# One hand-written order of tasks against another in a fused attention and GeGLU kernel: the early blocks, and where ScalarE sums a load of x

## The chip, the cores and the metric

The kernel runs on one core of a Trainium2 chip. The core has TensorE (matrix products into PSUM), VectorE, ScalarE and GpSimd, which work side by side, and SyncE, whose queue issues the DMAs. In the profile they are PE (PEld for TensorE's weight loads), DVE, ACT, POOL and SP. Each engine works through its own list of instructions in order; semaphores hold an instruction back until what it needs is there. The metric is the device time of one execution in microseconds: 183.78 us for the kernel before, the median of three runs (183.71 to 183.88).

## The reference

The input x has 2048 rows of 512 bf16 numbers. All that follows is added to it.

```python
x = A_x
xn = _layernorm(x, axis=-1)
return x + _A_ref(xn, A_wqkv, A_wo) + _B_ref(xn, B_w_gate, B_w_up, B_w_down)
```

`_A_ref` is attention with 32 heads of 16 dimensions. A row attends to 8 rows: itself and those 2, 4, ... 14 before it.

```python
W, dil = 8, 2
idx = pos[:, None] - off[None, :]          # off = arange(W) * dil
logits = jnp.einsum("bhsd,bhswd->bhsw", q, kg) * scale
logits = jnp.where(mask[None, None, :, :], logits, -1e9)
attn = _softmax(logits, axis=-1)
o = jnp.einsum("bhsw,bhswd->bhsd", attn, vg)
... @ wo
```

`_B_ref` is a feed-forward part with 1376 hidden columns:

```python
h = _gelu(xn @ w_gate) * (xn @ w_up)
return h @ w_down
```

## The kernel before

The rows are worked in four blocks b = 0 to 3 of 512 rows, each of two loads p = 2b, 2b+1 of 256 rows (`ld_x0` to `ld_x7`; the two of block 0 that come first are split in halves). Every piece of work is a task with a name, and a table, `ORDER` (lines 363 to 420), lists for each engine its tasks in the order in which they are issued. `Graph` works out from what tasks read and write which of them must wait for which. A planner, `Graph.schedule` (line 168), runs through these lists with assumed durations; it does not change the order, but it gives each task its buffer: the buffer of a pool that is free first by the plan. For a DMA the plan takes `nbytes` over an assumed rate, a fixed part and `lat` (lines 244 to 249). The buffers that matter here are the 8 banks of PSUM (pool `P_ps`), one for each matmul group until it has been evicted.

The tasks of a block, by name (the number after the name is the block, then parts of it):

- **Layer norm.** For the first four loads VectorE makes the statistics (`bnst`, `bnag`, `sub`, `norm`, numbered by tile of 128 rows), ScalarE the square root (`sq`). From the fifth load on (tiles 8 to 15), ScalarE does it: `bnst` t sums a tile (line 736), `ve`, `vp` make the mean, `bnag` t sums the squares (line 782), `va`, `vb` the variance, GpSimd the square root (`sq8` to `sq14`), VectorE the reciprocal (`rstd`), and ScalarE `sub` (line 813) and `norm` (line 820). Tiles 8 and 9 come from `ld_x4`, 10 and 11 from `ld_x5`, 12 and 13 from `ld_x6`.
- **Transposing.** Block 0 on TensorE (`tpx`, `tpy`, evicted by `evx` on ScalarE and `evy` on VectorE), the others by DMA transposes on SP's queue (`trx`, line 860).
- **Query, key and value.** Block 0 in small pieces (`mma`, `mmb`, `mmt`, `mmv`), evicted by ScalarE (`evq0`, `evk0`, `evv0`); later blocks `mm`b_which_g with which = 0, 1, 2 (line 1035), evicted at line 1046. `halo` and `halv` carry the last 16 keys and values to the next block.
- **Attention.** VectorE multiplies queries and shifted keys (`pr`b_0, `pr`b_1, line 1066), adds (`pa`, and `pb` for blocks 1 to 3); TensorE sums over the dimensions of a head (`er`, lines 1102 and 1109, which also makes the last 96 up columns); `mask` for block 0; ScalarE copies the logits (`lc`, line 1138); VectorE takes the maximum and subtracts it (`d1a` to `d2`); ScalarE `exp`, VectorE sums (`d4a` to `d4c`), ScalarE `ln` and `d5`, VectorE `d6`. Four stores (`ss`) and four loads (`sl`) on SP's queue spread the probabilities through memory. VectorE multiplies values and probabilities (`pv`, line 1217), adds (`pw`) and finishes with `pz`.
- **Feed-forward.** `fg` and `fu` on TensorE (line 1255), ten each, and `fg`b_10; ScalarE evicts them with `gelu` (line 1265, and 1302 for the last) and `uev` (line 1272, and 1310 for the pieces `uev`b_10a, b, c); VectorE multiplies (`h`, line 1279, and 1317 for `h`b_10).
- **Output.** `acc` on TensorE (line 1347) adds both parts in PSUM, `fe` on ScalarE evicts, `fin` on VectorE adds x again (loaded by `ldxr`), `sto` stores.

ScalarE holds one set of function tables at a time: square root at first, then gelu, with exp and ln in between for each block; each change is an ACT_TABLE_LOAD row. A `ldxr` of block b is issued after `gelu`b_5 (`G.order_after`, line 1335).

Of the kernel before, what the change touches and what calls it, by code (L numbers as in the profile page):

```python
# [96 lines left out]
class Graph:  # L97
# [250 lines left out]
    def report(self):  # L348
# [14 lines left out]
ORDER = {  # L363
    "pe":
        "warm0 warm1 warm2 warm3 warm4 warm5 warm6 warm7 warm8 warm9 tpx0_0 tpy0_0 warm10 warm11 warm12 "
        "warm13 warm14 mma0_0 tpx0_1 tpy0_1 mmb0_0 mma0_1 mmb0_1 mmt1_1 tpx1_0 mmt1_0 mmt1_2 tpx1_1 mmt0_2 "
        "mmv0_0 mmt1_3 mmt0_3 mmv0_1 fg0_0 fg0_1 fu0_0 fg0_2 fg0_3 fu0_1 fu0_2 mm1_1_2_0 mmv1_0 mm1_1_0_0 "
        "mm1_1_1_0 fg0_4 fu0_3 mm1_0_1_0 fu0_4 mm1_0_0_0 er0_3 fg0_10 fg0_5 fu0_5 mm1_0_2_0 fg1_0 mm1_0_3_0 "
        "fu1_0 mm1_1_3_0 fg1_1 fu1_1 mm1_2_0_0 fg0_6 fg1_2 fu0_6 mm1_2_2_0 fg0_7 fu1_2 fg1_3 fu1_3 mm1_2_1_0 "
        "fu0_7 fg1_4 fg1_5 mmv1_1 fg1_6 fg0_8 mm1_2_3_0 fu1_4 fu1_5 fu0_8 fu1_6 fg1_7 er1_3 fg1_8 fg1_9 fg0_9 "  # L370
        "fu0_9 fu1_7 mm2_0_1_0 fu1_8 fu1_9 mm2_0_0_0 mm2_1_3_0 mm2_1_0_0 mm2_0_3_0 mm2_1_2_0 mm2_0_2_0 "
        "mm2_1_1_0 fg2_0 fu2_0 accd1 fg2_1 fu2_1 fg2_2 accd2 fg1_10 fg2_3 mm2_2_2_0 fu2_2 fg2_4 fg2_5 acca0 "
        "accb0 fu2_3 er2_3 fu2_4 fu2_5 accd3 fg2_10 mm3_1_0_0 fg2_6 mm3_2_2_0 fg2_7 mm3_0_1_0 mm3_1_1_0 fu2_6 "
# [3 lines left out]
        "fu3_9 acca8 accb8 accd9 accd10 acca12 accd15_1 accb12 accd15_0 accd14_0 accd11 accd13 accw15_0 "  # L377
        "accw13 accw15_1 accw14_0 accw12 accd14_1 accw14_1 accd15_2 accw15_2",
    "act":
        "c_tbl sx1 sq0 negm1 sxx1 evx0_0 sq1 evx0_1 sq2 evq0_0 evq0_1 evx1_0 sq3 evk0_1 evk0_0 evk0_2 evx1_1 "  # L380
        "sq6 bnst8 evq0_2 bnst9 sq4 ve8 evk0_3 vp8 evq0_3 bnag8 evv0_0_0 bnag9 gelu0_1 gelu0_2 va8 vb8 "
        "gelu0_0 gelu0_3 evv0_0_1 uev0_0 uev0_1 evk1_2_0 uev0_2 evk1_0_0 halo1 evv0_1_0 evk1_1_0 gelu0_4 "
        "bnst10 uev0_3 bnst11 evq1_1_0 ve10 uev0_4 vp10 evq1_0_0 bnag10 uev0_10c lc0 uev0_10a gelu0_5 bnag11 "
        "uev0_5 va10 uev0_10b bnst12 exp0 evk1_3_0 evq1_3_0 uev1_0 ln0 d5_0 evq1_2_0 gelu0_10 vb10 gelu1_2 "
        "gelu1_1 sub8 evv1_2_0 sub11 uev0_6 uev1_1 norm8 gelu1_0 uev1_3 gelu0_7 uev1_2 sub10 sub9 uev0_7 "
        "gelu1_3 gelu0_6 gelu1_4 evv1_0_0 evv1_1_0 evv0_1_1 norm11 gelu1_6 gelu1_5 gelu0_8 norm10 uev1_5 "
        "bnst13 uev1_4 norm9 ve12 vp12 uev0_8 lc1 uev1_6 bnag12 bnag13 gelu0_9 uev0_9 gelu1_7 uev1_7 gelu1_9 "
        "gelu1_8 bnst14 va12 uev1_8 vb12 halv1 evv1_3_0 uev1_9 evq2_1_0 evk2_0_0 exp1 evq2_0_0 halo2 evk2_2_0 "
        "evq2_2_0 evk2_1_0 evk2_3_0 ln1 sub12 halv2 bnst15 ve14 vp14 uev1_10b evq2_3_0 fe1 d5_1 sub13 bnag14 "
        "bnag15 va14 vb14 halo3 uev1_10c uev2_0 gelu2_1 gelu2_2 norm12 sub15 evv2_2_0 sub14 fe2 gelu2_0 "  # L390
# [6 lines left out]
        "fe9 fe10 fe11 fe13 fe12",  # L397
    "dve":
        "c_wdz bnst0 bnag0 sub0 rstd0 norm0a norm0b mean1 sub1 evy0_0 rstd1 norm1a norm1b bnst2 bnag2 evy0_1 "
        "sub2 rstd2 norm2 bnst3 bnag3 sub3 rstd3 norm3 bnst7 bnst6 bnag7 bnag6 bnst4 sub6 rstd6 bnst5 norm6 "  # L400
        "bnag5 bnag4 sub7 sub5 rstd4 norm5 sub4 norm7 norm4 pr0_0 pr0_1 pa0 rstd8 h0_0 h0_1 mask d1a_0 d1b_0 "
        "d1c_0 d2_0 pr1_0 d4a_0 d4b_0 d4c_0 h0_2 d6_0 pr1_1 h0_10 pa1 h1_0 rstd10 pb1 h0_3 h1_1 pv0_0 pv0_1 "
        "d1a_1 h1_2 d1b_1 pw0_1 d1c_1 h0_4 d2_1 h1_4 pw0_2 d4a_1 pz0 d4b_1 d4c_1 h1_3 pr2_0 d6_1 pr2_1 fin1 "
        "rstd12 pa2 fin2 rstd14 pb2 h1_10 pv1_1 d1a_2 pv1_0 d1b_2 fin3 d1c_2 fin0 d2_2 h2_1 pw1_1 d4a_2 h2_10 "
        "h2_2 d4b_2 h2_0 d4c_2 pw1_2 d6_2 pz1 pr3_0 pr3_1 h2_3 pa3 pb3 fin5 pv2_0 d1a_3 d1b_3 d1c_3 d2_3 "
# [5 lines left out]
        "sq8 sq10 sq12 sq14",  # L411
    "sp":
        "ld_x0_0 ld_x0_1 ld_wq ld_x1_0 ld_wk ld_x3 ld_x1_1 ld_x2 ld_wv ld_x4 ld_wg0 ld_wu0 trx3_0 trx2_1 "
        "trx2_0 trx3_1 ld_wu1 ld_wg1 ld_wt0 ld_x5 ld_wt1 ld_wt2 ld_x6 ld_wd0 ldxr1 ss0_2 ss0_1 ss0_3 ss0_0 "
        "sl0_1 sl0_0 ld_x7 ld_wd1 trx4_0 sl0_3 ldxr2 ld_wo sl0_2 trx5_1 trx4_1 trx5_0 ss1_3 ss1_0 ss1_1 ss1_2 "
        "sl1_3 sl1_1 trx6_0 sl1_2 sl1_0 trx7_1 ldxr3 trx7_0 trx6_1 ldxr0 ldxr4 ss2_0 ss2_1 ss2_3 sto2 ss2_2 "
        "sl2_3 sl2_0 sto0 ldxr5 sl2_1 ldxr13 sto3 ldxr12 sl2_2 ldxr8 ldxr6 sto5 ldxr7 ldxr10 ss3_3 ss3_0 "
        "ss3_2 ss3_1 sl3_1 sl3_0 sl3_2 sl3_3 ldxr9 ldxr11 sto1 ldxr14 sto7 sto4 ldxr15 sto6 sto8 sto9 sto10 "
# [20 lines left out]
def bass_parallel_sum__sliding_local_dilated__glu_gated_geglu__prompt_kernel(nc, A_x, A_wqkv, A_wo, B_x, B_w_gate, B_w_up, B_w_down, out, dbg=None, cfg=None):  # L439
# [43 lines left out]
    with contextlib.ExitStack() as es:  # L483
        block = es.enter_context(nc.Block())

        def sb(name, shape, dt):
            return es.enter_context(nc.sbuf_tensor(name, shape, dt))
# [13 lines left out]
        mask = sb("mask", [32, 2, 4, 16], F32)  # L501
# [143 lines left out]
        for i, nm in enumerate(("q", "k", "v")):  # L645
            def mk(i=i):
                return lambda e: e.dma_start(
                    Wqkv[:, :, i * 512:(i + 1) * 512],
                    A_wqkv[:, i * 512:(i + 1) * 512].rearrange("(k p) n -> p k n", p=128))
# [4 lines left out]
        for (nm, Wx, I_w, src, h) in (("g", Wg, I_wg, B_w_gate, 0), ("u", Wu, I_wu, B_w_up, 0),  # L654
                                      ("g", Wg, I_wg, B_w_gate, 1), ("u", Wu, I_wu, B_w_up, 1)):
            def mk(Wx=Wx, src=src, c=slice(640 * h, 640 * h + 640)):
                return lambda e: e.dma_start(Wx[:, :, c], src[:, c].rearrange("(k p) n -> p k n", p=128))
            t_w = G.task("sp", "ld_w%s%d" % (nm, h), 0, mk(), wr=[(I_w, h)], prio=R_WG + (nm == "u") + 0.1 * h,
                         nbytes=(640, 1070)[nm == "g" and h == 0] * 1024)
            t_w.deps.add(t_ld["wk"])  # L660
            t_ld[nm] = t_w
        for (i, src, c0, c1, o) in ((0, B_w_gate, 1280, 1376, 32), (1, B_w_up, 1280, 1312, 0),
# [20 lines left out]
        def xp(it, p, t2):  # L683
            return [(it, (t2, 0)), (it, (t2, 1))] if p == 0 else [(it, t2)]
# [4 lines left out]
        for p in range(NP):  # L689
# [5 lines left out]
            if p < 2:  # L695
                for t2 in range(2):
                    def mk_ld(t2=t2, p=p, it=it_x):
                        return lambda e: e.dma_start(
                            XIN[:, it.slot, t2, :], x2[256 * p + 128 * t2:256 * p + 128 * t2 + 128, :])
                    t_x = G.task("sp", "ld_x%d_%d" % (p, t2), 0, mk_ld(), wr=xp(it_x, p, t2),  # L700
                                 prio=((-960, -959), (-957.8, -956.5))[p][t2], nbytes=128 * 1024)
            else:
                def mk_ld(p=p, it=it_x):
                    return lambda e: e.dma_start(
                        XIN[:, it.slot, :, :], x2[256 * p:256 * p + 256, :].rearrange("(t q) d -> q t d", q=128))
                t_x = G.task("sp", "ld_x%d" % p, 0, mk_ld(), wr=[(it_x, 0), (it_x, 1)],
                             prio=(0, 0, -897.5, -897)[p] if p < 4 else -950 + p * 20, nbytes=256 * 1024)
                if p >= 4:
                    G.order_after(t_x, t_ld["wv"])
            def tp0(t, b=b, base=base):  # L710
# [98 lines left out]
            for t2 in range(2):  # L809
# [33 lines left out]
                if t < 2:  # L843
                    for h in range(2):
# [5 lines left out]
                        nm = "norm%d%s" % (t, "ab"[h])  # L850
# [14 lines left out]
            for grp in ((0,), (1,)):  # L865
                n = len(grp)
                nm = "%d_%d" % (p, grp[0])
# [68 lines left out]
        for b in range(NB):  # L936
# [257 lines left out]
            for sj in range(4):  # L1194
                def mk_ss(sj=sj, itp=it_pb, b=b):
# [4 lines left out]
                       nbytes=60 * 1024)  # L1200
# [120 lines left out]
            for ti in range(4):  # L1321
# [15 lines left out]
                for ci, (c0, c1) in enumerate(cparts):  # L1337
# [59 lines left out]
                    def mk_so(t=t, it=it_ob, c0=c0, c1=c1, CW=CW):  # L1397
                        return lambda e: e.dma_start(out2[128 * t:128 * t + 128, c0:c1], OB[:, it.slot, 0:CW])
                    G.task("sp", "sto" + sfx, 0, mk_so(), rd=[it_ob], wr=[(I_out, (t, ci))], prio=base + 62,
                           nbytes=64 * CW)  # L1400
# [61 lines left out]
```

## Time and profile before

| what | value |
|---|---|
| median of 3 runs | 183.78 us |
| the profiled execution's own time | 183.74 us |
| its span, first to last instruction | 181.6 us |
| TensorE busy | 176.0 us (97%) |
| VectorE busy | 168.6 us (93%) |
| ScalarE busy | 133.0 us (73%) |
| GpSimd busy | 21.7 us (12%) |
| DMA queues' packets | 38.1% of 16 engines' span |
| granted TensorE clock | 1.00 |

The table's shares are averages over the span. A row of a timeline gives the start, the duration, the engine, the line of the kernel, the operation and the tiles (out<-in), how many instructions are merged in it, and in brackets the engine's idle time before it and what ended that. Times are counted from the span's start. Rows of windows give, for a stretch, its length, each engine's busy time with the number of instructions, the granted clock, the DMA engines' busy share and the GB/s.

### The profile page before, as it was taken

What the parts mean: (1) busy time and instruction counts of PE and PEld (TensorE: products, weight loads), DVE (VectorE), ACT (ScalarE), POOL (GpSimd) and SP (SyncE); (2) the same over time, 40 slices, a digit from 0 to 9 for tenths busy, and PEclk for the clock granted to TensorE, in tenths of its full rate; (3) what the DMA queues carried; (4) which work ended last, traced back from release to release, by engine and by line L of the source; (5) the groups of instructions that cost most, each with busy time, mean ns of one, the idle gap of its engine ahead of it and who ended that gap; (6) DMA issues with size and microseconds to landing.
All of it is one profiled execution on the core that took longest, in us unless ns stands there. A gap on an engine that the chain in (4) does not pass through costs nothing.

```text
span 181.6 us, 2768 instructions
## 1 busy us (share of the span) xinstructions
PE 176.0 (97%) x1043; PEld 90.8 (50%) x1060; DVE 168.6 (93%) x157; ACT 133.0 (73%) x270; POOL 21.7 (12%) x23
## 2 busy tenths in 40 slices
PE   8899999999999999999999999999999999999994
PEld 2797454434454445444444454444444444447454
DVE  3799997599999999999999999999999999999972
ACT  5689987999999998999986797953276686620110
POOL 6000450001400008707000000000000000000000
PEclk9999999999999999999999999999999999999999
DMA  4996799101496200002753000244160127710023
GB/s 121 363 357 146 135 312 299 58 23 30 107 222 216 58 4 0 0 0 60 168 153 70 24 22 0 72 112 137 26 202 8 58 58 205 256 59 4 0 72 101
DMA packets 27276, 19.60 MB, mean 108 GB/s; under 512 B 13856, under 2 KB 25088, under 8 KB 27264
## 3 DMA queue, kind: packets, MB, share of 16 engines
q1 hardware_dynamic: 27264, 19.44, 38.1%
q8 instruction: 8, 0.13, 0.3%
q14 instruction: 4, 0.03, 0.0%
HBM read 14.71 MB, written 3.15 MB: 98 GB/s over the span
## 4 chain that ended last, share of the span: by engine, by line
PE 76%; ACT 9%; DMA 6%; DVE 3%; SPq 3%; issue 1%; DVEq 0%
PE PS L1255 29%; PE PS L1347 28%; PE PS L1035 13%; DMA XIN<-in_A_x_dram 4%; DMA Wqkv<-in_A_wqkv_dram 2%; SPq L860 2%; PE PS L1294 1%; DVE st L717 1%; ACT XS L736 1%; PE PS L966 1%; ACT UU L1272 1%; ACT QT L1046 1%; PE PS L1102 1%; DVE XIN L840 1%; ACT XS L782 1%
## 5 line engine op out<-in xcount | busy, mean ns | idle before, releaser
L1347 PE MATMUL PS<-Wd,HT 128*128 128x512 bf16 (+2 forms) x206 | 40.2, 345 | 0.2
L1255 PE MATMUL PS<-xnT,Wu 128*128 128x512 bf16 x158 | 39.0, 379 | 0.2 <-issue 0.2
L1255 PE MATMUL PS<-xnT,Wg 128*128 128x512 bf16 x153 | 38.2, 379 | 0.5 <-ACT UU L1272 0.2
L1035 PE MATMUL PS<-xnT,Wqkv 128*128 128x512 bf16 x143 | 35.0, 379 | 0.8 <-ACT KT L1046 0.5
L1217 DVE TENSOR_TENSOR UNI<-VN,PT 128x8192 f16<-128x8192 bf16 x8 | 35.3, 4419 | 0.0
L1066 DVE TENSOR_TENSOR UNI<-QT,KT 128x8192 f16<-128x8192 bf16 x8 | 35.2, 4420 | 0.0
L1347 PEld LDWEIGHTS PS<-Wd,HT 128*128 128x128 bf16 x209 | 19.6, 98 | 19.0
L799 POOL TENSOR_TENSOR sq<-ve,mhalf 128x2 bf16<-128x2 f32 x4 | 18.8, 4699 | 63.8 <-ACT ve L795 63.8
L1272 ACT ACTIVATE UU<-PS 128x512 bf16<-128x512 f32 x40 | 23.8, 611 | 2.7 <-DVE HT L1279 1.4
L1380 ACT ACTIVATE OB<-PS 128x512 bf16<-128x512 f32 x14 | 8.3, 594 | 23.8 <-PE PS L1347 22.2
L1265 ACT ACTIVATE GG<-PS 128x512 bf16<-128x512 f32 x40 | 22.8, 616 | 3.2 <-PE PS L1255 2.7
L1255 PEld LDWEIGHTS PS<-xnT,Wu 128*128 128x128 bf16 x160 | 15.5, 98 | 19.1 <-ACT GG L1265 0.4
L1255 PEld LDWEIGHTS PS<-xnT,Wg 128*128 128x128 bf16 x160 | 15.6, 98 | 18.4 <-ACT nmean L767 0.4
L1035 PEld LDWEIGHTS PS<-xnT,Wqkv 128*128 128x128 bf16 x144 | 16.2, 114 | 16.2 <-ACT KT L1046 0.9
L1078 DVE TENSOR_TENSOR UNI<-UNI 128x8192 f16<-128x8192 f16 x4 | 17.7, 4419 | 0.0
L1226 DVE TENSOR_TENSOR UNI<-UNI 128x8192 f16<-128x8192 f16 x4 | 17.7, 4419 | 0.0
L1347 PE MATMUL PS<-Wo,OT 128*128 128x512 bf16 (+2 forms) x74 | 16.0, 344 | 0.1
L1279 DVE TENSOR_TENSOR HT<-GG,UU 128x1024 bf16<-128x1024 bf16 x20 | 13.3, 685 | 0.0
L1347 PEld LDWEIGHTS PS<-Wo,OT 128*128 128x128 bf16 x76 | 7.0, 98 | 6.7 <-DVE OT L1237 0.6
L1232 DVE TENSOR_TENSOR UNI<-UNI 128x4096 f16<-128x4096 f16 x4 | 9.2, 2290 | 0.1
L1046 ACT ACTIVATE KT<-PS 128x512 bf16<-128x512 f32 x12 | 7.0, 595 | 2.2 <-PE PS L1035 2.2
L1046 ACT ACTIVATE VN<-PS 128x512 bf16<-128x512 f32 x12 | 7.2, 616 | 1.9 <-PE PS L1035 1.9
(99 smaller groups left out, 180.4 us busy)
## 6 DMA issues: line engine op xcount, KB each, us to landing
PT<-pt_scratch SPq DMA_DIRECT2D x16, 256.0 KB, 4.4
out_dram<-OB SPq DMA_DIRECT2D x14, 128.0 KB, 2.0
XIN<-in_A_x_dram SPq DMA_DIRECT2D x12, 128.0 KB, 4.1
Wqkv<-in_A_wqkv_dram SPq DMA_DIRECT2D x3, 512.0 KB, 5.2
XIN<-in_A_x_dram SPq DMA_DIRECT2D x6, 256.0 KB, 5.3
Wg<-in_B_w_gate_dram SPq DMA_DIRECT2D x2, 640.0 KB, 7.3
Wu<-in_B_w_up_dram SPq DMA_DIRECT2D x2, 640.0 KB, 6.9
Wd<-in_B_w_down_dram SPq DMA_DIRECT2D x1, 1280.0 KB, 6.4
```

What stands on the lines that cost most here:

```text
L799: "pool", "sq%d" % t, 5.0, lambda e, t=t, n=n: e.tensor_tensor(out=sq[:, t:t + n], in0=ve[:, t:t + n], in1=mhalf[:, 0:n], op=ALU.pow),
L1035: ins = e.matmul(PS[:, 512 * it.slot:512 * it.slot + 512], lhsT=wcols(which, kt, g), rhs=xnT[:, itx.slot, kt, :], start=(kt == 0), stop=(k ...
L1046: return e.activation(out=o, in_=PS[:, 512 * it.slot:512 * it.slot + 512], func=ACTF.Identity, scale=(QSC, 1.0, 1.0)[which])
L1066: return lambda e: e.tensor_tensor(out=UNI[:, it.slot:it.slot + 2, :, :], in0=bass.AP(QT, (itq.slot * 4 + 2 * h) * 512, [[NQT * 4 * 512, 1 ...
L1078: return lambda e: e.tensor_tensor(out=UNI[:, i0.slot:i0.slot + 2, :, :], in0=UNI[:, i0.slot:i0.slot + 2, :, :], in1=UNI[:, i1.slot:i1.slo ...
L1217: return lambda e: e.tensor_tensor(out=bass.AP(UNI, ito.slot * 4096, [[NUNI * 4096, 128], [2048, 4], [512, 4], [1, 512]]), in0=bass.AP(VN, ...
L1226: return lambda e: e.tensor_tensor(out=UNI[:, i0.slot:i0.slot + 2, :, :], in0=UNI[:, i0.slot:i0.slot + 2, :, :], in1=UNI[:, i1.slot:i1.slo ...
L1255: ins = e.matmul(PS[0:M, 512 * it.slot:512 * it.slot + 512], lhsT=Wx[:, kt, j * 128:j * 128 + M], rhs=xnT[:, itx.slot, kt, :], start=(kt = ...
L1265: return lambda e: e.activation(out=GG[:, ito.slot, q, :], in_=PS[:, 512 * it.slot:512 * it.slot + 512], func=ACTF.Gelu_apprx_tanh)
L1272: return lambda e: e.activation(out=UU[:, ito.slot, q, :], in_=PS[:, 512 * it.slot:512 * it.slot + 512], func=ACTF.Identity)
L1279: return lambda e: e.tensor_tensor(out=HT[:, ito.slot, j - 1:j + 1, :], in0=GG[:, ig.slot, :, :], in1=UU[:, iu.slot, :, :], op=ALU.mult)
L1347: ins = e.matmul(PS[:, 512 * it.slot:512 * it.slot + CW], lhsT=(OT[:, ito.slot, q, ti * 128:(ti + 1) * 128] if kind == "o" else HT[:, ith. ...
```

## The change

On TensorE, ScalarE, VectorE and SP the same tasks stand in another order. On TensorE the orders differ from the task after `mmt1_0` up to `er1_3`, on VectorE from `bnst4` up to `pv0_0`, on ScalarE from `evk0_0` up to `ve12`, on SP from the task after `ld_wt2` up to `ss1_3`. ScalarE's sums `bnst10` and `bnst11` over the load `ld_x5` stand later, behind `gelu0_5`; `gelu0_10` stands ahead of `exp0`; `sub8`, `sub9` and `norm8` stand earlier. On SP, `ld_x6` stands behind `ss0_2`, and the weights `ld_wd0`, `ld_wd1`, `ld_wo` and the load `ld_x7` ahead of it. Apart from that, two assumed numbers of the planner change (the bytes of four weight loads and a `lat` for the loads from `ld_x5` on); no DMA moves other bytes.

```diff
@@ ORDER["pe"]
-        "warm13 warm14 mma0_0 tpx0_1 tpy0_1 mmb0_0 mma0_1 mmb0_1 mmt1_1 tpx1_0 mmt1_0 mmt1_2 tpx1_1 mmt0_2 "
-        "mmv0_0 mmt1_3 mmt0_3 mmv0_1 fg0_0 fg0_1 fu0_0 fg0_2 fg0_3 fu0_1 fu0_2 mm1_1_2_0 mmv1_0 mm1_1_0_0 "
-        "mm1_1_1_0 fg0_4 fu0_3 mm1_0_1_0 fu0_4 mm1_0_0_0 er0_3 fg0_10 fg0_5 fu0_5 mm1_0_2_0 fg1_0 mm1_0_3_0 "
-        "fu1_0 mm1_1_3_0 fg1_1 fu1_1 mm1_2_0_0 fg0_6 fg1_2 fu0_6 mm1_2_2_0 fg0_7 fu1_2 fg1_3 fu1_3 mm1_2_1_0 "
-        "fu0_7 fg1_4 fg1_5 mmv1_1 fg1_6 fg0_8 mm1_2_3_0 fu1_4 fu1_5 fu0_8 fu1_6 fg1_7 er1_3 fg1_8 fg1_9 fg0_9 "
+        "warm13 warm14 mma0_0 tpx0_1 tpy0_1 mmb0_0 mma0_1 mmb0_1 mmt1_1 tpx1_0 mmt1_0 mmt0_2 tpx1_1 mmt1_2 "
+        "mmt1_3 mmt0_3 mmv1_0 mmv0_1 fg0_0 fg0_1 fg0_2 fg0_3 fu0_0 mmv0_0 fg0_4 mm1_0_0_0 mm1_1_0_0 mm1_0_1_0 "
+        "mm1_1_1_0 mm1_0_2_0 fu0_1 fu0_2 fu0_3 fg0_5 er0_3 mm1_0_3_0 fu0_4 mm1_1_3_0 fg0_10 mm1_1_2_0 fg1_0 "
+        "fu0_5 fg1_1 fu1_0 fg0_6 fg1_2 fu1_1 fg0_7 fg1_3 fu0_6 fu0_7 mm1_2_0_0 fu1_2 fu1_3 fg1_4 mmv1_1 fu1_4 "
+        "fg1_5 mm1_2_1_0 mm1_2_2_0 fu1_5 mm1_2_3_0 fg0_8 fg1_6 fu0_8 fg1_7 fu1_6 er1_3 fg1_8 fg1_9 fg0_9 "
@@ ORDER["act"]
-        "c_tbl sx1 sq0 negm1 sxx1 evx0_0 sq1 evx0_1 sq2 evq0_0 evq0_1 evx1_0 sq3 evk0_1 evk0_0 evk0_2 evx1_1 "
-        "sq6 bnst8 evq0_2 bnst9 sq4 ve8 evk0_3 vp8 evq0_3 bnag8 evv0_0_0 bnag9 gelu0_1 gelu0_2 va8 vb8 "
-        "gelu0_0 gelu0_3 evv0_0_1 uev0_0 uev0_1 evk1_2_0 uev0_2 evk1_0_0 halo1 evv0_1_0 evk1_1_0 gelu0_4 "
-        "bnst10 uev0_3 bnst11 evq1_1_0 ve10 uev0_4 vp10 evq1_0_0 bnag10 uev0_10c lc0 uev0_10a gelu0_5 bnag11 "
-        "uev0_5 va10 uev0_10b bnst12 exp0 evk1_3_0 evq1_3_0 uev1_0 ln0 d5_0 evq1_2_0 gelu0_10 vb10 gelu1_2 "
-        "gelu1_1 sub8 evv1_2_0 sub11 uev0_6 uev1_1 norm8 gelu1_0 uev1_3 gelu0_7 uev1_2 sub10 sub9 uev0_7 "
-        "gelu1_3 gelu0_6 gelu1_4 evv1_0_0 evv1_1_0 evv0_1_1 norm11 gelu1_6 gelu1_5 gelu0_8 norm10 uev1_5 "
-        "bnst13 uev1_4 norm9 ve12 vp12 uev0_8 lc1 uev1_6 bnag12 bnag13 gelu0_9 uev0_9 gelu1_7 uev1_7 gelu1_9 "
+        "c_tbl sx1 sq0 negm1 sxx1 evx0_0 sq1 evx0_1 sq2 evq0_0 evq0_1 evx1_0 sq3 evk0_0 evk0_1 evx1_1 evq0_2 "
+        "sq6 bnst8 evk0_2 evk0_3 sq4 bnst9 evq0_3 ve8 evv0_1_0 vp8 evv0_0_1 bnag8 gelu0_0 bnag9 gelu0_2 va8 "
+        "sub8 vb8 gelu0_1 sub9 evq1_0_0 gelu0_4 evk1_0_0 evv0_0_0 gelu0_3 evq1_1_0 evk1_1_0 halo1 evq1_2_0 "
+        "uev0_0 uev0_1 uev0_2 uev0_3 norm8 gelu0_5 bnst10 uev0_10c lc0 evq1_3_0 bnst11 uev0_10b evk1_3_0 "
+        "uev0_10a gelu0_10 exp0 uev0_4 ve10 evk1_2_0 uev0_5 ln0 vp10 d5_0 gelu1_1 bnag10 gelu1_2 gelu0_6 "
+        "bnag11 gelu0_7 va10 uev1_1 vb10 uev0_6 gelu1_3 uev1_2 uev0_7 gelu1_0 uev1_3 uev1_0 sub11 evv0_1_1 "
+        "bnst12 gelu1_5 uev1_4 gelu1_4 evv1_1_0 evv1_2_0 uev1_5 bnst13 evv1_0_0 sub10 norm11 gelu0_8 norm10 "
+        "gelu1_6 norm9 ve12 vp12 uev0_8 lc1 uev1_6 bnag12 bnag13 gelu0_9 uev0_9 gelu1_7 uev1_7 gelu1_9 "
@@ ORDER["dve"]
-        "sub2 rstd2 norm2 bnst3 bnag3 sub3 rstd3 norm3 bnst7 bnst6 bnag7 bnag6 bnst4 sub6 rstd6 bnst5 norm6 "
-        "bnag5 bnag4 sub7 sub5 rstd4 norm5 sub4 norm7 norm4 pr0_0 pr0_1 pa0 rstd8 h0_0 h0_1 mask d1a_0 d1b_0 "
-        "d1c_0 d2_0 pr1_0 d4a_0 d4b_0 d4c_0 h0_2 d6_0 pr1_1 h0_10 pa1 h1_0 rstd10 pb1 h0_3 h1_1 pv0_0 pv0_1 "
+        "sub2 rstd2 norm2 bnst3 bnag3 sub3 rstd3 norm3 bnst7 bnst6 bnag7 bnag6 bnst5 sub6 rstd6 bnst4 norm6 "
+        "bnag5 bnag4 sub7 sub5 rstd4 norm5 sub4 norm7 norm4 pr0_0 pr0_1 pa0 rstd8 h0_1 h0_0 mask d1a_0 d1b_0 "
+        "d1c_0 d2_0 pr1_0 d4a_0 d4b_0 d4c_0 h0_10 h0_2 d6_0 pr1_1 pa1 h1_1 h0_3 h1_0 pb1 rstd10 pv0_0 pv0_1 "
@@ ORDER["sp"]
-        "trx2_0 trx3_1 ld_wu1 ld_wg1 ld_wt0 ld_x5 ld_wt1 ld_wt2 ld_x6 ld_wd0 ldxr1 ss0_2 ss0_1 ss0_3 ss0_0 "
-        "sl0_1 sl0_0 ld_x7 ld_wd1 trx4_0 sl0_3 ldxr2 ld_wo sl0_2 trx5_1 trx4_1 trx5_0 ss1_3 ss1_0 ss1_1 ss1_2 "
+        "trx2_0 trx3_1 ld_wu1 ld_wg1 ld_wt0 ld_x5 ld_wt1 ld_wt2 ldxr1 ld_wd0 ld_wd1 ld_wo ld_x7 ss0_2 ldxr2 "
+        "ld_x6 ss0_1 ss0_3 ss0_0 sl0_1 sl0_0 sl0_2 sl0_3 trx5_1 trx4_0 trx4_1 trx5_0 ss1_3 ss1_0 ss1_1 ss1_2 "
@@ the planner's numbers
-                         nbytes=(640, 1070)[nm == "g" and h == 0] * 1024)
+                         nbytes=((630, 1070), (960, 900))[h][nm == "g"] * 1024)
...
+                t_x.lat = 1.5 if p >= 5 else 0.0
```

## The prediction, made before the changed kernel was run

> **What bounds the kernel now.** I began with busy time by stretches, to see where TensorE isn't full; its stages are the stretches.
>
> ```profile
> core 0: us, PE busy (x) PEld busy (x) DVE busy (x) ACT busy (x) POOL busy (x), PEclk, DMA share, GB/s
> 5.00:32.00 27.00, 26.29 (x266) 18.27 (x270) 24.63 (x44) 23.12 (x58) 4.68 (x1) 1.00 0.92 268
> 32.00:40.00 8.00, 8.00 (x38) 3.59 (x35) 5.95 (x6) 7.82 (x16) 0.00 (x0) 1.00 0.12 36
> 40.00:46.00 6.00, 5.23 (x24) 2.37 (x25) 5.61 (x7) 5.94 (x13) 1.40 (x1) 1.00 0.14 33
> 46.00:60.00 14.00, 13.95 (x69) 6.83 (x68) 14.00 (x9) 14.00 (x30) 1.56 (x1) 1.00 0.64 172
> 60.00:175.00 115.00, 114.16 (x600) 55.15 (x612) 114.45 (x84) 78.05 (x151) 11.16 (x2) 1.00 0.25 69
> ```
>
> TensorE is full from 6 us on except in 40 to 46, where 0.77 us are missing; its granted clock is 1.00 everywhere. VectorE is full from 42 us on. Then TensorE's timeline there:
>
> ```profile
> 39.01 1.03 PE L1255 MATMUL PS<-xnT,Wu 128*128 128x512 bf16 x4
> 40.49 1.05 PE L1035 MATMUL PS<-xnT,Wqkv 128*128 128x512 bf16 x4 [0.45 <-ACT KT L1046]
> ...
> 44.40 1.05 PE L1035 MATMUL PS<-xnT,Wqkv 128*128 128x512 bf16 x4 [0.27 <-ACT GG L1302]
> ```
>
> Idle time understates a stall, as ends of matmuls are modelled. Each task raises its engine's semaphore when it ends, and the trace has those moments; I use them as ends throughout. Four matmuls of 512 columns come 0.864 us after the task before when nothing stalls. mm1_2_0 came after 1.51, so it lost 0.64; mm1_2_2 after 1.32, so 0.46. Together 1.10. Every other task from 7 us to the end keeps its pace; the four er tasks, or what follows them, lose 0.09 each. So TensorE's stream can be shortened by 1.10 us and no more.
>
> What the two waited for is found by counting. PSUM has 8 banks, so the k-th task that takes a bank needs the (k-8)-th release, and ScalarE's order of evictions sets the releases. Counted so in the order before, mm1_2_0 needs evk1_3 (ended 40.44) and mm1_2_2 needs gelu0_10 (44.35): just the names in brackets. TensorE's stream resumes 0.25 us after a release (40.44 to 41.55-0.864, 44.35 to 45.47-0.864). Why they were late is in ScalarE's timeline:
>
> ```profile
> 26.47 0.60 ACT L1265 ACTIVATE GG<-PS 128x512 bf16<-128x512 f32 x1
> 28.30 0.63 ACT L736 ACTIVATE XS<-XIN 128x512 bf16<-128x512 bf16 x1 [1.23 <-DMA XIN<-in_A_x_dram]
> ...
> 32.89 1.03 ACT L1138 ACTIVATE PB<-PS 128x1024 bf16<-128x1024 f32 x1
> ...
> 37.59 1.28 ACT L1160 ACT_TABLE_LOAD   x1
> 38.89 1.06 ACT L1161 ACTIVATE EX<-PB 128x1024 f16<-128x1024 bf16 x1
> ...
> 42.45 1.28 ACT L1302 ACT_TABLE_LOAD   x1
> 43.74 0.60 ACT L1302 ACTIVATE GG<-PS 128x512 bf16<-128x512 f32 x1
> ```
>
> bnst10, the sum over the load x5, stood early and held ScalarE 1.23 us; lc0 (PB), exp0 and gelu0_10 all followed late. VectorE paid too:
>
> ```profile
> 31.35 0.29 DVE L1132 TENSOR_TENSOR PS<-PS,mask 32x128 f32<-32x128 f32 x1 [0.86 <-PE PS L1109]
> 33.95 0.43 DVE L1143 TENSOR_TENSOR SU<-PB 128x512 bf16<-128x512 bf16 x1 [2.31 <-ACT PB L1138]
> ...
> 41.98 0.69 DVE L1187 TENSOR_TENSOR PB<-EX,rc 128x1024 bf16<-128x1024 f16 x1 [0.32 <-ACT rc L1183]
> ```
>
> At the end the two engines run side by side: pz3 ends at 173.74 on VectorE, and accw15_0, which needs it, follows accd13 (173.94) on TensorE with 0.03 lost. A gain of TensorE alone would stop there at about 0.2; both must gain.
>
> **The change, walked along the new orders** with ends from the rows: an eviction 0.49 back to back and 0.62 after a wait, a half UT copy 0.40, a sum 0.62, a square 0.70, sub and norm 0.61, a small one 0.09 to 0.20, lc0 1.03, table plus exp 2.37, table plus gelu 1.91. Nothing is added or removed.
>
> *To 16 us.* mmt0_2 starts at 10.53, and evx1_0 (10.27 plus 0.25) just meets it, as it met mmt1_2 before. evk0_0 now waits for mmt1_0 (10.53) and ends 11.16, evk0_1 11.64, evx1_1 12.28; mmt1_3 would start at 12.54, which 12.28 plus 0.25 just meets (0 to 0.1 lost; I take 0). evq0_3 ends 15.88 against 15.84, still before norm4 (16.11) frees VectorE: pr0_0, pr0_1 and pa0 stay, pa0 at 29.23. The swap of bnst4 and bnst5 shifts no end that counts; sq4 at 14.74 is in time for rstd4.
>
> *16 to 30 us.* ScalarE: evv0_0_1 17.0, gelu0_0 19.6, gelu0_2 20.8, vb8 21.7, gelu0_1 22.2, sub9 22.8, evq1_0 23.6, evk1_1 26.6, evq1_2 27.2, then the uev0 as fu0 ends, uev0_3 29.66. sq8 on GpSimd takes 4.76 after vb8, so 26.4, before rstd8 at 29.31 on VectorE. TensorE needs the releases 2 us or more after they come; mm1_0_0 starts at 22.1 and the transposes of its block landed at 20.68; er0_3 starts at 29.9 and ends at 31.33 in both kernels, after pa0. sub8, sub9 and norm8 (1.83 us of ScalarE) now fill the time of the waits.
>
> *30 to 46 us.* norm8 30.27, gelu0_5 30.76, bnst10 31.38 (x5 landed at 28.27, no wait), uev0_10c 31.8, lc0 32.83 instead of 33.92. evq1_3, bnst11, uev0_10b 34.3, evk1_3 34.8; uev0_10a waits for fg0_10 (34.87) and ends 35.49; gelu0_10 36.0, now before exp0, which ends 38.4 instead of 39.96. VectorE: d2_0 34.61, pr1_0 38.94, d4c 39.99. ScalarE: uev0_5 39.95, ln0 40.34, d5 40.72, table and gelu1_1 42.63, gelu1_2 43.82, gelu0_6 44.31, gelu0_7 45.50, uev1_1 46.08. Against TensorE, with 0.25 added: fu0_6 needs gelu1_1 (42.88) and starts at 43.50; fu0_7 needs gelu1_2 (44.07), 44.36; mm1_2_0 needs gelu0_6 (44.56), 45.23; fu1_2 needs gelu0_7 (45.75), 46.09; fu1_3 needs uev1_1 (46.33), 46.96; later ones have 0.8 and more. The least slack is 0.29. Both stalls go: 1.10.
>
> One rule speaks against it. A table costs the row's 1.28, and ScalarE stands idle 0.03 around it. The Trainium skill ("ScalarE: Activation LUTs", section "What ACT_TABLE_LOAD costs") puts 1.38 us of drain on top of each switch; by it gelu1_2 would end some 2.7 later and TensorE would lose 2.4, which gives 185.0. The row shows no such drain, and I go by the row.
>
> *VectorE.* h0_10 moves ahead of d6_0 into time that was idle; h0_2 ends 40.92, d6_0 41.52, pr1_1 45.85, pa1 50.18 instead of 51.69, pb1 and rstd10 54.25, so pv0_0 starts 1.5 earlier than 55.76. Its multiplicands: uev1_3 49.1 for h1_1, uev1_0 49.6 for h1_0, evv0_1_1 50.7, all before use. rstd10, now behind pb1, is wanted by norm11 at about 56.
>
> *SP's queue.* ld_wd0, ld_wd1, ld_wo and ld_x7 stand behind ldxr1, which waits for gelu0_5 (30.8): 2.1 MB that at the 268 GB/s of the first stretch take 8 us, gone by 40; their first readers are after 75 us. ss0_2 waits for d6_0 and is followed by ldxr2 and ld_x6 before the other three stores: 1.1 us of issue (0.59 and 0.5), so the stores end their issue at 45.35 as before (41.56+2.65+1.1), and sl0_0, which landed at 52.12, has until 54.25. ld_x6 is issued by 43.4 and lands by 50.5 with the longest x load of the trace (7.06); bnst12 wants it at 50.7. What stood behind them, trx4_0 to trx5_0, ends at about 62.9 and is wanted by mm2_0_1 at 65.3.
>
> *The planner's numbers* (bytes, lat) move no byte; they only enter the plan that gives out banks and buffers. With releases in ScalarE's order the count above holds for any such plan; only an aligned pair for er1_3 could bind otherwise (it lost nothing before).
>
> *Sum.* From 60 us the orders are the same and all engines stand 1.1 or more earlier. 183.74 (the profiled execution, 0.04 under the median) less 1.10 is 182.64; I say 182.65.
>
> **Rivals.**
> *ScalarE is later than walked.* Slack is 0.29 at fu0_7 and 0.34 at fu1_2. With every row from uev0_10a at its slow end (evictions 0.62, squares 0.85, small ones 0.2 to 0.24), gelu1_2 ends at 44.8 and gelu0_7 at 46.9: 1.03 lost, 183.67. For it: two tables and eight dependences lie there; against: ScalarE ran such stretches back to back. Likely size 0.2 to 1.0: 182.85 to 183.65.
> *The end is set elsewhere, the gain given back.* If VectorE gained under 0.4, TensorE would wait for pz3: about 183.4 to 184.1. Against: VectorE is walked 1.5 ahead and had no idle time from 42.7 to 173.7.
> *Slower: the probabilities' way through memory.* Three stores now follow 384 KB of loads. It binds once sl0_0 lands after 54.25, and gives a loss over 0.2% once pv0_0 starts after 56.3 (55.76, the 0.2 at the end and 0.37), 4.2 later than sl0_0 landed before. The stores end their issue where they did; if none of the loads' time overlaps it and they move at the 106 GB/s that 45 to 50 us had, they add 3.6: 55.7, which leaves about 183.5. Under 92 GB/s it is slower than before; at half of 106, pv0_0 starts at 59.3, 3.3 lost, 187. Against: the loads are issued before the three stores, and such a load lands 5.3 after its issue at the median, ldxr in 2.6, so most of it is over by 46. The Trainium skill ("DMA: Bandwidth & Descriptors", section "Queues, rings and completion order") has descriptors consumed in ring order, which would put the loads wholly ahead; no row here separates it.
>
> **How the numbers follow.** As walked 0.62 (182.45 to 182.95); ScalarE late 0.17, of which 0.05 within 0.2% of before; given back 0.08, same; slower 0.13. 0.2% is 0.37 us, about what a measurement of this kernel can tell from no change. Faster 0.74, same 0.13, slower 0.13. The lower end is the full gain and 0.2 of spread at the end; the upper, 183.6, takes in the slow-end walk and leaves under 2 in 10 out.
>
> **What would show it.** Right: no idle bracket on TensorE in 36 to 48; ScalarE's sum of x5 without the DMA wait; PB's copy starting near 31.8, exp's table near 36.0, gelu's near 40.7; VectorE's first pv near 54.3; span near 180.5. Wrong: brackets on TensorE naming GG L1265 near 44 to 46, VectorE waiting on PT, ScalarE waiting on XIN near 50, or an idle bracket on Wo's matmuls at the end.

## The result, and the profile after

The changed kernel takes 182.53 us (median of six runs, 182.35 to 182.84) against 183.83 us for the kernel before: a ratio of 0.9926 with a 95% interval of 0.9906 to 0.9945, 1.3 us less. Run again later beside two experiments it gave 182.72 us against 183.94 (0.9938, 0.9924 to 0.9953). The profiled execution took 182.4 us, with a span of 180.3 us.

Busy time by the same stretches, of the changed kernel; line numbers of the kernel are one higher than before from line 709 on.

```profile
core 0: us, PE busy (x) PEld busy (x) DVE busy (x) ACT busy (x) POOL busy (x), PEclk, DMA share, GB/s
...
32.00:40.00 8.00, 8.00 (x39) 3.76 (x38) 7.15 (x10) 7.87 (x16) 0.00 (x0) 1.00 0.84 282
40.00:46.00 6.00, 6.00 (x30) 2.76 (x29) 5.97 (x5) 5.97 (x16) 0.00 (x0) 1.00 0.43 107
```

TensorE is full from 40 to 46, where 0.77 us were missing, and VectorE has 7.15 instead of 5.95 us of work from 32 to 40. TensorE's timeline where the two stalls were:

```profile
40.59 1.03 PE L1256 MATMUL PS<-xnT,Wu 128*128 128x512 bf16 x4
41.45 1.89 PE L1256 MATMUL PS<-xnT,Wg 128*128 128x512 bf16 x8
43.18 1.89 PE L1256 MATMUL PS<-xnT,Wu 128*128 128x512 bf16 x8
44.91 1.03 PE L1036 MATMUL PS<-xnT,Wqkv 128*128 128x512 bf16 x4
```

No row has an idle bracket, and the starts follow one another by 0.86 us for each four matmuls. By the ends of tasks nothing on TensorE loses more than 0.02 after 8.1 us except the 0.09 to 0.11 behind each of the four er tasks. ScalarE's timeline of the changed kernel:

```profile
30.00 0.59 ACT L1266 ACTIVATE GG<-PS 128x512 bf16<-128x512 f32 x1
30.48 0.63 ACT L737 ACTIVATE XS<-XIN 128x512 bf16<-128x512 bf16 x1
...
31.62 1.02 ACT L1139 ACTIVATE PB<-PS 128x1024 bf16<-128x1024 f32 x1
...
35.40 0.60 ACT L1303 ACTIVATE GG<-PS 128x512 bf16<-128x512 f32 x1
36.01 1.28 ACT L1161 ACT_TABLE_LOAD   x1
37.31 1.06 ACT L1162 ACTIVATE EX<-PB 128x1024 f16<-128x1024 bf16 x1
...
40.47 1.28 ACT L1266 ACT_TABLE_LOAD   x1
41.77 0.60 ACT L1266 ACTIVATE GG<-PS 128x512 bf16<-128x512 f32 x1
```

The sum over x5 (XS, at 30.48) follows an eviction without a wait for a DMA; the logits' copy (PB) starts at 31.62 instead of 32.89, exp's table at 36.01 instead of 37.59, gelu's at 40.47 instead of 42.45. VectorE:

```profile
32.68 0.42 DVE L1144 TENSOR_TENSOR SU<-PB 128x512 bf16<-128x512 bf16 x1 [1.21 <-ACT PB L1139]
...
41.19 4.42 DVE L1067 TENSOR_TENSOR UNI<-QT,KT 128x8192 f16<-128x8192 bf16 x1
...
54.07 4.41 DVE L1218 TENSOR_TENSOR UNI<-VN,PT 128x8192 f16<-128x8192 bf16 x1
```

Its wait for the logits is 1.1 us shorter, and pv0_0 starts at 54.07 instead of 55.67.

Where the time went, by the ends of tasks in the two traces. The last matmul ends at 177.97 instead of 179.27, 1.30 sooner. Of that, 1.10 are the two stalls (0.64 and 0.46), 0.03 the loss at accw15_0, and 0.17 the start: mma0_0 ended at 6.68 instead of 6.85, since the first weights landed at 5.92 instead of 6.09. The orders are the same up to there, so the 0.17 is not of the change: between these two traces the change is worth 1.13 us.

### The profile page after: what moved, and what is told of

It is laid out like the page before. It is cut to its first block, busy times and chain, and to the rows that moved or that the text cites. A ratio compares the mean times of both kernels' runs of the same rounds, so it can differ in the third digit from the quotient of the medians.

```text
span 180.3 us, 2783 instructions
## 1 busy us (share of the span) xinstructions
PE 176.3 (98%) x1060; PEld 91.0 (50%) x1060; DVE 168.8 (94%) x157; ACT 132.7 (74%) x270; POOL 20.0 (11%) x23
## 4 chain that ended last, share of the span: by engine, by line
PE 95%; DMA 2%; SPq 0%; issue 0%; DVE 0%; DVEq 0%
PE PS L1256 38%; PE PS L1348 29%; PE PS L1036 17%; PE PS L953 3%; DMA Wqkv<-in_A_wqkv_dram 2%; PE PS L1011 2%; PE PS L1295 2%; PE PS L1103 1%; PE PS L1110 1%; PE PS L967 1%; SPq L698 0%; PE PS L878 0%; DVE OB L1392 0%; PE PS L889 0%; DVEq L335 0%
## 5 line engine op out<-in xcount | busy, mean ns | idle before, releaser
L1256 PE MATMUL PS<-xnT,Wg 128*128 128x512 bf16 x160 | 39.0, 379 | 0.0
L1036 PE MATMUL PS<-xnT,Wqkv 128*128 128x512 bf16 x144 | 34.4, 379 | 0.0
L800 POOL TENSOR_TENSOR sq<-ve,mhalf 128x2 bf16<-128x2 f32 x4 | 17.1, 4282 | 64.1 <-ACT ve L796 64.1
```

Source lines behind the costliest of these rows:

```text
L800: "pool", "sq%d" % t, 5.0, lambda e, t=t, n=n: e.tensor_tensor(out=sq[:, t:t + n], in0=ve[:, t:t + n], in1=mhalf[:, 0:n], op=ALU.pow),
L1036: ins = e.matmul(PS[:, 512 * it.slot:512 * it.slot + 512], lhsT=wcols(which, kt, g), rhs=xnT[:, itx.slot, kt, :], start=(kt == 0), stop=(k ...
L1256: ins = e.matmul(PS[0:M, 512 * it.slot:512 * it.slot + 512], lhsT=Wx[:, kt, j * 128:j * 128 + M], rhs=xnT[:, itx.slot, kt, :], start=(kt = ...
```

## The experiments

The theory was the prediction's: ScalarE's early wait for x5 made its evictions late, TensorE stood twice for a PSUM bank, VectorE was late by the same cause, and the end needs both engines. The rivals were that the new orders as such make the gain (the gelu task ahead of exp0 above all), that SP's queue does, or that TensorE's stream alone sets the time. All times below are medians. "Walked" is what was added up along an order beforehand; a task "loses" what its end comes later, after the end of the task before it, than at its pace without a stall. In the rows of e1 and e2 the line numbers are those of the kernel before, in e3 to e7 those of the changed kernel; in e8 they are 6 higher than before, in e9 and e10 7.

**The wait alone, on the kernel before.** e1 puts the sum later, e2 the load earlier.

```diff
 e1, ORDER["act"]
- gelu0_4 bnst10 uev0_3 bnst11 evq1_1_0 ve10 uev0_4 vp10
+ gelu0_4 uev0_3 evq1_1_0 bnst10 uev0_4 bnst11 ve10 vp10
 e2, ORDER["sp"]
- trx2_0 trx3_1 ld_wu1 ld_wg1 ld_wt0 ld_x5 ld_wt1
+ trx2_0 trx3_1 ld_x5 ld_wu1 ld_wg1 ld_wt0 ld_wt1
```

> The kernel before with one edit: on ScalarE bnst10 stands behind evq1_1 and bnst11, ve10 behind uev0_4, nothing else moves. Theory (the two bank stalls come from ScalarE's wait for the load x5): ScalarE no longer waits for x5, but it still has both sums, vp10 and bnag10 ahead of lc0; walked, lc0 ends at 33.35 instead of 33.92, evk1_3 at 39.9, gelu0_10 at 43.6, so mm1_2_0 still loses about 0.1 and mm1_2_2 about 0.3 of the 0.64 and 0.46; VectorE gains about 0.6; the time is 0.6 to 0.8 under before, 183.1. Rival (the reordering as a whole makes the gain, the wait is only a part of idle time that costs nothing): within 0.2 of before, 183.8.

> The kernel before with one edit: on SP's queue ld_x5 stands behind trx3_1, ahead of ld_wu1, so that x5 lands some 3 us sooner; ScalarE's, TensorE's and VectorE's orders are those of before. Theory: bnst10 starts at 27.1 without a wait, lc0 ends at about 32.95, evk1_3 at 39.4 (0.4 before mm1_2_0 needs it, with 0.25 of latency) and gelu0_10 at 43.2 (43.45 against 43.51): both stalls go, VectorE's d6_0 comes 1.1 sooner, and the time is 1.0 to 1.1 under before, 182.7, nearly all of what the new orders brought. Rival (the orders themselves are needed, gelu0_10 ahead of exp0 above all): 183.3 to 183.8.

e1 took 183.29 us against 183.78 before (0.9973, 0.9956 to 0.9989), e2 182.70 (0.9932, 0.9907 to 0.9956). ScalarE in e2:

```profile
26.23 0.60 ACT L1265 ACTIVATE GG<-PS 128x512 bf16<-128x512 f32 x1
26.72 0.62 ACT L736 ACTIVATE XS<-XIN 128x512 bf16<-128x512 bf16 x1
...
41.08 1.28 ACT L1302 ACT_TABLE_LOAD   x1
42.38 0.60 ACT L1302 ACTIVATE GG<-PS 128x512 bf16<-128x512 f32 x1
```

x5 landed at 22.48 instead of 28.27; the sum follows the eviction directly, and gelu0_10 ends at 42.98 instead of 44.35. Neither stall is left on TensorE. So one load's place in the queue, with all three compute orders of before, brings nearly all that the reordering brings (from the end of mma0_0 to the last matmul 1.07 us less than before, against 1.13): the wait for x5 is the cause, and gelu0_10 ahead of exp0 is not needed for the gain. e1 brought less than walked (0.5, not 0.6 to 0.8; in its trace TensorE gains 0.30). ScalarE no longer waits for x5, but part of that wait comes back as two waits for TensorE's products:

```profile
27.28 0.60 ACT L1272 ACTIVATE UU<-PS 128x512 bf16<-128x512 f32 x1 [0.27 <-PE PS L1255]
28.15 0.60 ACT L1046 ACTIVATE QT<-PS 128x512 bf16<-128x512 f32 x1 [0.27 <-PE PS L1035]
```

Both sums still stand ahead of lc0, which ends at 33.58 instead of the 33.35 walked (33.92 before); evk1_3 ends at 40.09 and gelu0_10 at 44.01. TensorE:

```profile
40.14 1.05 PE L1035 MATMUL PS<-xnT,Wqkv 128*128 128x512 bf16 x4
...
44.05 1.05 PE L1035 MATMUL PS<-xnT,Wqkv 128*128 128x512 bf16 x4 [0.27 <-ACT GG L1302]
```

mm1_2_0 loses 0.34 instead of 0.64, mm1_2_2 still 0.46: TensorE came to it as much sooner as gelu0_10 did.

**The wait put into the changed kernel.**

```diff
 e3, ORDER["act"]
- evk1_1_0 halo1 evq1_2_0 uev0_0 uev0_1 uev0_2 uev0_3 norm8 gelu0_5 bnst10 uev0_10c
+ evk1_1_0 halo1 bnst10 evq1_2_0 uev0_0 uev0_1 uev0_2 uev0_3 norm8 gelu0_5 uev0_10c
```

> The changed kernel with one task put back early: bnst10 behind halo1 on ScalarE, where it must wait for x5 (landed at 28.2) from 26.5 on. Theory: ScalarE loses 1.7 there and gets 0.4 back from later waits; lc0 ends at about 33.9, exp0 at 39.2, gelu1_1 at 43.65; fu0_6 and fu0_7 lose about 0.9 together for banks; VectorE is 1.2 later and pz3 then holds TensorE's last tasks: 1.0 to 1.1 over the changed kernel, 183.6, so the place of this one sum carries the gain. Rival (the new orders have slack for it): under 0.3 over the changed kernel.

e3 took 183.53 us, no longer distinguishable from the kernel before on the same chip (0.9996, 0.9977 to 1.0016). ScalarE and TensorE of e3:

```profile
28.25 0.63 ACT L737 ACTIVATE XS<-XIN 128x512 bf16<-128x512 bf16 x1 [1.59 <-DMA XIN<-in_A_x_dram]
```

```profile
43.77 1.04 PE L1256 MATMUL PS<-xnT,Wu 128*128 128x512 bf16 x4 [0.29 <-ACT GG L1266]
```

fu0_6 loses 0.47 and fu0_7 0.32 (walked: about 0.9 together); with 0.08 at accd1 and 0.03 at accw15_0, TensorE gives back 0.90 of the 1.13. The place of this one sum carries most of the gain by the trace, and all that can be told apart by the times.

**gelu0_10, the tables and h0_10.** e4 puts two tasks back where they were, e5 one of them, e6 the other with h0_10 as early as it can then stand.

```diff
 e4 and e6, ORDER["act"]
- uev0_10a gelu0_10 exp0 uev0_4 ve10 evk1_2_0 uev0_5 ln0 vp10 d5_0 gelu1_1
+ uev0_10a exp0 uev0_4 ve10 evk1_2_0 uev0_5 ln0 vp10 d5_0 gelu0_10 gelu1_1
 e4 and e5, ORDER["dve"]
- d4c_0 h0_10 h0_2 d6_0 pr1_1 pa1
+ d4c_0 h0_2 d6_0 pr1_1 h0_10 pa1
 e6, ORDER["dve"]
- d4c_0 h0_10 h0_2 d6_0 pr1_1 pa1
+ d4c_0 h0_2 d6_0 h0_10 pr1_1 pa1
```

> The changed kernel with gelu0_10 behind d5_0 on ScalarE, as before the change (so exp0 starts 0.6 sooner and gelu0_10's bank is held 6 us longer), and h0_10 behind pr1_1 on VectorE. Theory by counting banks: gelu0_10 ends at about 41.9 and is the release that fg1_3 needs at 42.5, gelu1_1 ends at 42.4, so TensorE waits for nothing; VectorE's sum of work is the same; the time is that of the changed kernel within 0.15, 182.5. Rival (the place of gelu0_10 against the two table loads is what removed the stalls): a stall named GG near 42 to 45 and 0.4 or more over the changed kernel.

e4 took 185.47 us against 183.78 for the kernel before (1.0082, 1.0057 to 1.0106), 2.9 us over the changed kernel: not the theory, and by its waits not the rival either. In its trace mm1_2_0 lost 1.54, fu1_2 0.31 and er1_3 1.06. ScalarE's gelu0_6 had waited 1.8 us for h0_10 on VectorE. There are three gelu buffers (GG, each for two products), and I had moved the task that gives one back. So e5 and e6 parted the two edits.

> The changed kernel with one task moved: h0_10 behind pr1_1 on VectorE, where it stood before the change; ScalarE's order, gelu0_10 ahead of exp0, stays. Theory (from e4: gelu0_10's buffer is one of three gelu buffers, h0_10 gives it back, and gelu0_6 is the task that needs it): gelu0_6 ends at about 46.2 instead of 44.0, mm1_2_0 loses about 1.4 and fu1_2 0.3 for banks, pb1 is late for er1_3 by about 1, and the time is that of e4, 185.4. Rival (the order of the tables did it in e4, this place is free): 182.5.

> The changed kernel with gelu0_10 behind d5_0 on ScalarE as in e4, but h0_10 between d6_0 and pr1_1 on VectorE. Theory: h0_10 waits for gelu0_10 (42.6), so VectorE stands idle for 1.2 us and everything after it is 1.2 to 1.6 later; gelu0_6 has its buffer at 43.0 and TensorE loses nothing between 40 and 50 us; TensorE waits at accw15_0 for pz3, and the time is 1.1 to 1.5 over the changed kernel, 183.8: the tables' order costs only through h0_10. Rival (gelu0_10 late holds a PSUM bank that TensorE needs): TensorE idle with GG near 42 to 46.

e5 took 184.43 us against 183.61 (1.0040, 1.0025 to 1.0055). Its ScalarE and TensorE rows:

```profile
42.94 0.58 ACT L1266 ACTIVATE GG<-PS 128x512 bf16<-128x512 f32 x1
45.92 0.60 ACT L1266 ACTIVATE GG<-PS 128x512 bf16<-128x512 f32 x1 [2.40 <-DVE HT L1318]
```

```profile
46.57 1.05 PE L1036 MATMUL PS<-xnT,Wqkv 128*128 128x512 bf16 x4 [1.53 <-ACT GG L1266]
```

gelu0_6 waits 2.40 for its buffer, mm1_2_0 then loses 1.72 for its bank and fu1_2 0.31: 1.9 us over the changed kernel for the place of a 0.33 us task. It was 1.0 less than expected, as er1_3 lost nothing here. e6 took 184.31 us (1.0034, 1.0024 to 1.0044), 0.5 more than walked. VectorE waited as expected, TensorE lost its time elsewhere than expected:

```profile
42.42 0.42 DVE L1318 TENSOR_TENSOR HT<-GG,UT 128x512 bf16<-128x512 bf16 x1 [1.22 <-ACT GG L1303]
```

```profile
60.68 0.62 PE L1103 MATMUL PS<-xnT,Wt 128*32 128x256 bf16 x16 [1.65 <-ACT UU L1273]
```

Nothing is lost between 40 and 50 us beyond 0.08, so gelu0_10's own bank is not the trouble; but er1_3 stands 1.7 us for an eviction of an up product. That is uev0_8. er1_3 needs an aligned pair of banks, and the planner had chosen another pair: in the changed kernel and e5 banks 6 and 7, given back by evv1_0 and gelu0_8; in e4 and e6 banks 0 and 1, given back by gelu0_8 and uev0_8.

**The pair of banks by itself.** e9 keeps every order of the changed kernel and dictates two choices of the planner; e10 dictates one to e6.

```diff
 e9 and e10, Graph.schedule
+                c = [x for x in c if x[1] == PIN.get(it.name, x[1])]
+                if not c:
+                    return None
                 k = min(c)[1]
+PIN = {"u0_8": 7, "lg1": 6}      e9
+PIN = {"g0_8": 5}                e10
```

> The changed kernel, all orders unchanged; the planner is told to give fu0_8 bank 7 and er1_3's logits the pair 6 and 7, so that the pair is released last by uev0_8 (59.7) instead of gelu0_8 (57.2), as the plan of e4 and e6 had it. Theory (what e4 and e6 lost at er1_3 is the pair that the plan chose, and not the order of the tables): er1_3 loses 1.0 for uev0_8, VectorE is untouched (lc1 still ends before d1a_1 wants it), and TensorE's stream sets the end 1.0 later: 183.5. Rival (VectorE's lateness made er1_3 late in e4 and e6, the pair is free): 182.5.

> e6 with fg0_8 put into bank 5, so that er1_3's pair is released by uev1_5 and gelu0_8 as in the changed kernel. Theory: TensorE loses nothing at er1_3, VectorE is still 1.6 later through h0_10's wait for gelu0_10, so the 1.7 that e6 lost at er1_3 come back only as far as VectorE allows: TensorE waits some 1.4 for pz3 at accw15_0 instead, and the time is 183.95, 0.2 to 0.4 under e6. Rival (TensorE's loss at er1_3 was all of e6): the changed kernel's 182.5.

e9 took 183.51 us against 182.72 for the changed kernel beside it. Its TensorE row:

```profile
60.03 0.62 PE L1109 MATMUL PS<-xnT,Wt 128*32 128x256 bf16 x16 [0.83 <-ACT UU L1279]
```

er1_3 loses 0.90 for uev0_8, where 1.0 was expected. VectorE is on time up to d1a_1, as expected, but is not left alone after that: lc1 and exp1 end 0.90 later, and d4a_1 waits for exp1 (in the changed kernel the same instruction, at 72.51, has no wait in brackets):

```profile
73.72 0.43 DVE L1176 TENSOR_TENSOR SU<-EX 128x512 f16<-128x512 f16 x1 [0.97 <-ACT EX L1168]
```

So both engines end 0.9 later. That wait comes 13 us after er1_3's, so VectorE's lateness did not make the loss at er1_3: the pair costs 0.9 by itself. The 1.72 at this place in e6 are more, as uev0_8 itself ended later there (60.64, against 59.99 in e9): in e6 ScalarE waits 0.7 for a gelu buffer that late VectorE gives back.

e10 took 183.79 us against 184.31 for e6, 0.5 less where 0.2 to 0.4 was walked. Its pair is banks 4 and 5, given back by uev1_5 and gelu0_8; the expectation has these as the tasks of the changed kernel too, where it is evv1_0 and gelu0_8, but gelu0_8 is the last in both. er1_3 loses nothing, and TensorE loses 0.09 at fg1_3, 0.35 at fg0_8, 0.74 at accd1 and 0.03 at accw15_0. The 0.35 comes from the dictated bank: evv1_2 gives it back at 55.14, and fg0_8's four matmuls end 1.10 after that, the usual 0.86 and about 0.25. I had expected all of VectorE's lateness to show at accw15_0; it showed at accd1, the first task that takes attention's output from VectorE (pz0, which ended at 75.78). The time is 1.1 over the changed kernel, where 1.4 was walked: late tables cost through h0_10's wait on VectorE.

**SP's queue.** e7 is the changed kernel with the whole SP order of before.

```diff
 e7, ORDER["sp"]
- ld_wt2 ldxr1 ld_wd0 ld_wd1 ld_wo ld_x7 ss0_2 ldxr2 ld_x6 ss0_1 ss0_3 ss0_0 sl0_1 sl0_0 sl0_2 sl0_3 trx5_1 trx4_0 trx4_1
+ ld_wt2 ld_x6 ld_wd0 ldxr1 ss0_2 ss0_1 ss0_3 ss0_0 sl0_1 sl0_0 ld_x7 ld_wd1 trx4_0 sl0_3 ldxr2 ld_wo sl0_2 trx5_1 trx4_1
```

> The changed kernel with SP's whole order of before. Theory: the queue's order is free on both sides: ld_x6 and ld_wd0 earlier hinder nothing, sl0_2 lands by 57 and pv0_1 wants it at 58.5; the time is that of the changed kernel within 0.15, 182.5. Rival (the store-and-load way of the probabilities gained from the loads that no longer stand between sl0_0 and sl0_2): 0.3 or more over the changed kernel, with VectorE waiting on PT.

182.52 us (0.9935 of the kernel before, 0.9917 to 0.9952), the changed kernel's time. sl0_0 landed at 50.78, in the changed kernel at 52.97: the loads among the stores cost it 2.2 us, and VectorE wanted it at 54.1. Counted from the end of d6_0, which the stores wait for, it is 2.2 in this trace of the changed kernel and 3.0 in that of e11. In the changed kernel the two loads landed at 44.60 and 45.67, and the three stores behind them from 45.90 to 47.72; in e7 the same stores landed from 44.19 to 45.47.

**More work on VectorE.**

```diff
 e8, ORDER["dve"] (dum0, dum1: EX = EX + EX, 128x1024)
- pw3_2 pz3
+ pw3_2 dum0 dum1 pz3
```

> The changed kernel with two more additions of 128x1024 fp16 on VectorE between pw3_2 and pz3, on a buffer that nothing reads any more (some 1.2 us of work; nothing is left out). Theory (VectorE has about 0.15 of slack at the end, so a gain of TensorE alone would have been worth that much): TensorE waits at accw15_0 and the time is 1.0 to 1.1 over the changed kernel, 183.6. Rival (TensorE's stream alone sets the time): within 0.2 of the changed kernel, 182.5.

e8 took 183.23 us beside e7's 182.52, and TensorE waits at the end:

```profile
173.45 3.00 PE L1353 MATMUL PS<-Wo,OT 128*128 128x256 bf16 x19 [0.89 <-DVE OT L1243]
```

accw15_0 loses 1.06 of the 1.2 us that were added, so the slack was near 0.15. The median rose by 0.7 only. Span against span the two traces differ by 1.0 (181.3 and 180.3), but the profiled execution of e8 had 1.8 us outside its span where the others have 2.0 to 2.1; what that is stays open.

> The changed kernel itself, beside the two others on one chip: 182.5, and its trace again for how much the start varies (the end of mma0_0 lay between 6.43 and 6.90 in the traces so far).

182.72 us, and mma0_0 ended at 6.86.

## Why the prediction was right

The forecast was 182.65 us, the result 182.53. The mechanism is the one forecast; that the two agree to 0.12 is in part luck, as the start alone moves a trace by more than that. Step by step:

- *Two stalls of 1.10 on TensorE are all there is to win.* Right: both are gone and nothing else moved on TensorE but 0.03 at the end. The remaining 0.17 of the traces' difference is the start.
- *They come from ScalarE's wait for x5.* Shown from three sides: e2 takes the wait away and gains 1.07 of 1.13, e3 puts it back and loses 0.90, and e1, which takes the wait away but leaves both sums ahead of lc0, gains 0.30.
- *The walk.* Predicted and measured ends: lc0 32.83 and 32.66, gelu0_10 36.0 and 36.01, exp0 38.4 and 38.37, gelu1_1 42.63 and 42.37, gelu0_7 45.50 and 45.23, pa1 50.18 and 50.08. The trace began 0.17 sooner, and within 0.2 of that these ends lie where they were put. sq8 on GpSimd, put at 26.4, ended at 25.18; it is wanted only at 29. The rival of a later ScalarE didn't come true.
- *The table rule.* The row was the better guide: in the changed kernel too ScalarE stands idle 0.02 around a load of 1.28, and the table with gelu1_1 takes 1.91. The 1.38 of drain that the Trainium skill adds to each switch ("ScalarE: Activation LUTs", section "What ACT_TABLE_LOAD costs") is in none of these traces. By the prediction's estimate from it the time would have been 185.0.
- *VectorE must gain too.* Right by e8, and by e10, where its lateness costs 1.1. In e8 VectorE's slack at the end was 0.15, so without its own gain TensorE's would have been lost but for about that.
- *SP's queue costs nothing.* Right by e7. The bound for the loads among the stores was 0 to 3.6 us; it is 2.2, hidden by 1.1 (54.1 less 53.0) in this trace, and 3.0, hidden by only 0.2, in e11's, where sl0_0 landed at 54.03 and pv0_0 started at 54.25.
- *The planner's numbers change nothing.* With the old numbers the planner gives every task the same buffer and the same waits. The reservation that an aligned pair for er1_3 could bind was more than a form of words: it bound in e4, e6 and e9, by 0.9 to 1.7.

One step was too small, without harm to the sum. I valued h0_10's new place at the 0.33 us of idle VectorE time that it fills. By e5 it holds 1.9 us: h0_10 and h0_2 give back the gelu buffers for gelu1_2 and gelu0_6, which have both moved forward, and with h0_10 behind pr1_1 the second of the two buffers comes only at 45.90. The prediction counts PSUM banks along the new orders, but not gelu buffers.

## What to carry to other kernels

When an engine works through a written order, count releases: number the tasks that take a buffer of a pool of n, and the k-th needs the (k-n)-th release in the order of the engine that empties it, as long as each takes the buffer that comes free first (e10's dictated bank broke that, and cost 0.35). Done for the kernel before, the count names the stalls that the trace shows, which checks it; done for the new order, with durations from the rows, it says which go. Do it for every pool, the small SBUF ones too, and for pairs, since a task that looks idle may be the one that gives the buffer back.

Look first at the queue that feeds the waiting engine: here one load issued ahead of three weight loads (e2) did nearly as much as a new order on four engines.

## What the runs showed that was not expected

The start varies from trace to trace with the same instructions: over the thirteen traces mma0_0 ended between 6.43 us (e8) and 7.03 us (e10), with the first weights landing between 5.67 and 6.27. By the end of fg0_0 the spread is 16.69 to 17.12, as TensorE lost 0.14 and 0.17 again right after the two earliest starts (e7 and e8). Since TensorE has no slack later, this goes straight into the time; that it makes most of the spread of a kernel's runs (0.5 us for the changed kernel) is likely, but only the profiled runs show their start.

In e3, e10 and e11 the last warm-up matmuls of 128 columns took 0.11 us each instead of 0.06, and in e3 and e11 mma0_0 ended 1.06 and 0.99 after its weights had landed instead of 0.76. The records of the granted clock fit this: the full clock is first recorded at 5.92 us in e10 and at 6.52 in e11, and at 3.66 to 5.10 in the other traces (e3 has no record). Why it came later there was not tried.
